# A recurrence beside a feed-forward layer: y and the state's products of steps six to eleven put into one place

## The chip, the core and the metric

The kernel runs on one core of a Trainium2 chip. The time is device time in microseconds (us) of the whole program, and a lower time is better. The engines of a core work on their own instruction streams, each in the order of its program, and wait for each other through semaphores: TensorE (PE in the profile, with its weight loads as PEld), VectorE (DVE), ScalarE (ACT), GpSimd (POOL), and SyncE (SP), which only starts DMA transfers here.

## The reference

There are two blocks. The first is a recurrence with a decay for every channel: 4 batches, 8 heads, 768 time steps, 48 channels a head.

```python
for t in range(S):
    cur = einsum('bhd,bhe->bhde', u * k[t], v[t])
    y[t] = einsum('bhd,bhde->bhe', r[t], state + cur)
    state = w[t][..., None] * state + einsum('bhd,bhe->bhde', k[t], v[t])
```

The second is a feed-forward layer on y, brought to 3072 tokens of 384 channels, with 2048 hidden channels:

```python
h = x @ w_in
g = h * erf(softplus(h))
out = g @ w_out
```

Everything is fp32.

## The kernel before

**The work is cut into twelve steps.** A step takes one chunk of 128 tokens of two batches, all heads. Even steps belong to one pair of batches, odd steps to the other, so a pair's state goes from step s to step s + 2. A chunk is two halves of 64 tokens, and in each the recurrence is worked out by levels: level n makes the part of the 64 x 64 table of token pairs that lies between neighbouring blocks of 2^(n-1) tokens, with r and k scaled by running products of the decays (`scale`, L364 in this path). The table is called `own`. From step five on, levels one to four come from VectorE and GpSimd on another layout (the rest of `prepare`, L486 to L568, "the row work"), and only levels five and six come from TensorE (`level_products`, L671). `take_level` brings a level from PSUM into `own`: level five by a predicated copy on VectorE (L681), level six by two copies on ScalarE (L688).

**y of a step comes in three parts**, all added up in one PSUM tile `y`: `from_own` (L703) multiplies `own` with v, once for each of two arrangements of the heads (swap 1 and swap 0); `through_state` (L729) adds r through the state at the chunk's start (S) and at its middle (`middle`). Between the two arrangements stands a fence: VectorE copies a few elements of `y` (L712), and the second arrangement has to wait for that copy. After that ScalarE copies `y` out (L737, L758), and SP's DMAs (L764) bring the last 16 channels of each into place, giving the layer's input xT. y of step s - 1 is finished in step s.

**The state** is advanced in two halves. `state_part` (L778) multiplies k (`kT`, multiplied beforehand by decays, L837) with v for both halves; then middle = faded S + first product (L857) and next state = faded middle + second product (L863), on VectorE. The fading, a multiplication with the chunk's decays, is GpSimd's (L832, L860), and both use one buffer, `faded`. kT comes by DMA (L617) from a copy in DRAM, behind two other transfers in SP's order (L609, L611), and is then multiplied by `spread`, decays that come by DMA (L802, L807) from products that TensorE makes with level six (L791).

**The feed-forward layer fills the rest.** In each step, TensorE computes the output projection of step s - 3 in seven products (P, L1275, each 8 matmuls of 128 x 192) and the hidden layer of step s - 1 in eight pieces (H, L1153, each 12 matmuls of 128 x 256). ScalarE copies the pieces out (L1162) and computes softplus (s, L1109) and erf (e, L1113); VectorE multiplies (m, L1118) and makes the blends that the projection uses (S1 to S4, L1252 to L1258). Two outputs are added on VectorE (L1295, L1300), and they free the PSUM buffers `m` that the hidden pieces then use.

**The order is written out by hand** in `attend_late` and in lists of tokens that it runs at named places:

```python
STAGES_LATE = ("front", "near", 0, 1, 2, 3, 4)
USUAL = ("s P", "m", "ey P m s P P ep P", "m k22y P F P k11p F F",
         "S1", "S2 S3 H k12y S4 H F", "s H ey m H H F s H ep H H")
```

F and `next(following, None)` advance the row work of the next step by one piece, up to its next `yield`. Each engine then takes its instructions in the order in which the program issues them.

**PSUM** has two banks of products in this path. Level five, level six with the spread, and the state's products all take bank 0 (`products(..., 0)`, called pp_107 or pp in the profile), one after the other; bank 1 serves ScalarE as a place for erf and copies.

Of the kernel before, what the change touches and what calls it, by code (L numbers as in the profile page):

```python
# [17 lines left out]
P = 128  # L18
# [3 lines left out]
HC = 64  # L22
NC = 2
# [17 lines left out]
DIRECT = 4  # L41
NEAR_LOG = 4
NEAR = 1 << NEAR_LOG
LOG = 6
# [47 lines left out]
def kernel(  # L92
# [14 lines left out]
    nc = tc.nc  # L107
    PSUM = bass.MemoryType.PSUM

    n_steps, _, _, JP, C = rkw.shape  # L110
    NH, D = v.shape[2:]
    NP = JP // NJ
    NE = NH // JP
# [5 lines left out]
    SPC = NB // NJ  # L119
# [20 lines left out]
    middle = const.tile([P, JP, D], FP32, name="middle")  # L140
    faded = [const.tile([P, JP, D], FP32, name="faded")] * NC
# [22 lines left out]
    def products(shape, n=None):  # L164

        if n is None:
            n = turns["next"]
            turns["next"] = 1 - n
        names = "abc"[: len(shape) - 1]
        return banks[n][:].rearrange(  # L170
            f"p ({' '.join(names)}) -> p {' '.join(names)}", **dict(zip(names, shape[1:]))
        )

    loaded = {}
# [165 lines left out]
    both = slice(0, EP + D)  # L340
# [7 lines left out]
    def scale(s, level, batch=None):  # L348

        in_t, tots = loaded[s][0], ready[s][1]  # L350
        half, nb = 1 << (level - 1), JP * C >> level
        if batch is not None:
            nb //= NJ
            halves = view(
                turns["first"][:, batch], half, [[NP * C - half, 2], [2 * half, nb], [1, half]]
            )
            nc.vector.tensor_mul(
                halves, halves,
                view(tots[level - 1], 2 * batch * nb, [[1, 2], [2, nb], [0, half]]),
            )  # L360
            return
        n = 1 if s > DIRECT and level == LOG else 2
        halves = view(in_t[:, 0:2], half, [[JP * C - half, n], [2 * half, nb], [1, half]])
        nc.vector.tensor_mul(  # L364
            halves, halves, view(tots[level - 1], 0, [[1, n], [2, nb], [0, half]])
        )
# [23 lines left out]
    def prepare(s):  # L390


        in_t = loaded[s][0]
        if s < DIRECT:
            rk1 = att.tile([P, 2, JP, C], FP32, name="rk1", bufs=1)
            ready[s] = (rk1,)
            parts = 1 if s else NJ
            def multiply_u(i, x):
                n = slice(i * JP // parts, (i + 1) * JP // parts)
                with_u, plain = (  # L400
                    [
                        t.rearrange("p n (t two) -> p n t two", two=2)[..., one]
                        for t in (rk1[:, x, n], in_t[:, x, n] if s else turns["first"][:, i, x])
                    ]
                    for one in (x, 1 - x)
                )
                if not s and not (x and not i):
                    nc.vector.tensor_mul(
                        with_u[0], with_u[1],
                        u_sb[:, :, None].to_broadcast([P, NP, C // 2]),  # L410
                    )
                    nc.vector.tensor_copy(out=plain[0], in_=plain[1])
                    return
                for p in range(NP):
                    of = slice(p, None, NP)
                    nc.scalar.mul(
                        out=with_u[0][:, of], in_=with_u[1][:, of], mul=u_sb[:, p : p + 1]
                    )
                nc.scalar.copy(plain[0], plain[1])

            if s < 2:
                for i in range(parts):
                    for x in range(2):
                        multiply_u(i, x)
                return
            yield
            yield
            multiply_u(0, 0)
# [21 lines left out]
        own = att.tile([P, NH, HC], FP32, name="own")  # L450
# [116 lines left out]
        fade(beside, k, 1)  # L567
        nc.vector.tensor_mul(own_terms, own_terms, r)  # L568
        fade(nc.vector, r, 1)
        if levels < NEAR_LOG:  # L570
            yield
        sum_up(1)
        multiply(nc.vector, 2)
# [103 lines left out]
    def take_level(own, pp, level):  # L677
        half = 1 << (level - 1)
        got = pp[:].rearrange("p e n t -> p (e n) t")
        if level <= MASKED:  # L680
            nc.vector.copy_predicated(  # L681
                rights(own[:], half),
                rights(mask_sb[:, level - 1 : level, :].to_broadcast([P, NH, HC]), half),
                got[..., : HC // 2].rearrange("p n (b h) -> p n b h", h=half),
            )
        else:
            for s0 in range(0, C, HC):
                nc.scalar.copy(own[s0 : s0 + half, :, half:], got[s0 : s0 + half, :, :half])  # L688
# [5 lines left out]
    def from_own(s, own, swap):  # L694
        vt = loaded[s][1]
        for j in range(NJ):
            for q in range(0, NP, 2):
                for h in range(NC):
                    e = h ^ swap
                    for p in (q, q + 1):  # L700
                        n = j * NP + p
                        t = slice(h * HC, (h + 1) * HC)
                        nc.tensor.matmul(  # L703
                            y[at(e, p), e, p // 2, j, t],
                            lhsT=vt[t, n * NE + e, :], rhs=own[t, e * JP + n, :],
                            start=swap == 1 and not j and not q, stop=True,
                            skip_group_check=True,
                        )
# [60 lines left out]
    def state_part(s, kT, ps, halves=None):  # L769

        vt = loaded[s][1]
        if halves is None:
            halves = range(1 if s >= n_steps - SPC else NC)
        for n in range(JP):
            for h in halves:
                for e in range(NE):
                    t = slice(h * HC, (h + 1) * HC)
                    nc.tensor.matmul(  # L778
                        ps[h][e][rows(e), n, :D],
                        lhsT=kT[t, e * JP + n, :],  # L780
                        rhs=vt[t, n * NE + e, :],
                        start=True,
                        stop=True,
                    )
# [27 lines left out]
    def attend_late(s, run):  # L812

        c, in_t, vt, own, S, S_next, ends = parts_of(s)
        RK = by_pair(in_t)
        before = s - 1 if s - 1 > DIRECT else None
        if before:
            from_own(before, ready[before][0], 1)
            fence()
        pp = products([P, NE, JP, HC], 0)  # L820
        level_products(pp, RK, LOG - 1)
        scale(s, LOG - 1)
        take_level(own, pp, LOG - 1)
        run("front", None)
        if before:
            from_own(before, ready[before][0], 0)
            through_state(before, xTs[before])
            if s + 1 < n_steps:
                load_step(s + 1)
        following = prepare(s + 1) if s + 1 < n_steps else iter(())  # L830
        next(following, None)
        nc.gpsimd.tensor_mul(faded[0][:], S[:], ends[:, :, 0:1].to_broadcast([P, JP, D]))  # L832
        next(following, None)
        run("near", None)
        next(following, None)
        kT = kTs[s]
        nc.vector.tensor_mul(  # L837
            kT[:].rearrange("p (e n) d -> p n e d", e=NE),
            kT[:].rearrange("p (e n) d -> p n e d", e=NE), spread[s][:],
        )  # L840
        run(0, following)

        pp = products([P, NE, JP, HC], 0)
        level_products(pp, RK, LOG)
        if s + 1 < n_steps:
            spread_blocks(s + 1, pp)
        take_level(own, pp, LOG)
        if s > DIRECT + 1:
            scale(s, LOG)
        run(1, following)  # L850
        if s == DIRECT + 1:
            scale(s, LOG)
        ps = products([P, NC, JP, HC], 0)
        ps = [[ps[:, h]] * NE for h in range(NC)]
        state_part(s, kT, ps)
        run(2, following)
        nc.vector.tensor_add(middle[both], faded[0][both], ps[0][0][both, :, :D])  # L857
        run(3, following)
        if s < n_steps - SPC:
            nc.gpsimd.tensor_mul(  # L860
                faded[1][:], middle[:], ends[:, :, 1:2].to_broadcast([P, JP, D])
            )
            nc.vector.tensor_add(S_next[both], faded[1][both], ps[1][0][both, :, :D])  # L863
        run(4, following)

    def attend_first(xT):
# [674 lines left out]
    with tc.manual_schedule(  # L1541
# [15 lines left out]
        for s in range(n_steps):  # L1557
# [44 lines left out]
            def run(n, following):  # L1602
                if n == 3 and s < n_steps - 2:
                    load_rows(s + 2)
                if n == 3 and s + 3 < n_steps:
                    load_w(s + 3)
                run_late(s, LATE.get(s, USUAL)[STAGES_LATE.index(n)], following)
# [120 lines left out]
```

## Time and profile before

| | us |
|---|---|
| median of 3 runs | 575.22 (575.20 to 575.34) |
| the profiled execution | 574.36 |
| its span, first to last instruction | 572.6 |
| TensorE busy in the span | 564.2 |
| VectorE, ScalarE, GpSimd busy | 452.7, 358.5, 246.8 |

The granted TensorE clock was 0.999 of full speed. Steps six to ten run from 232.7 to 454.25 us of the span, and step eleven from there to 477.8. In step seven (277.06 to 321.36) TensorE was busy for 44.30 us, VectorE for 37.41, ScalarE for 29.24 and GpSimd for 22.93.

In the profile, a row names the line, the engine, what was written and from what; "x64" counts instructions, and an fp32 matmul is two. The chain that ended last follows the work back from the last instruction to the first, so its rows, in order of time, tell what the time was spent on. A wait row reads: engine, what it was to write and its line, the releaser and its line, then the us in total, how often, and the longest. Times in the text are from the span's start.

### The profile page before, as it was taken

The numbers are of one execution on the slowest core, as the hardware profiler recorded it, in microseconds if no ns is written. First come the engines' busy times: TensorE is split into PE (matmuls) and PEld (weight loads), VectorE is DVE, ScalarE is ACT, GpSimd is POOL, SyncE is SP. The second block draws the span as 40 slices with busy tenths as digits, with TensorE's granted clock in tenths as the row PEclk, the third lists the DMA queues.
The fourth block names the chain that finished last, engine by engine and source line by source line (L and its number), as shares of the span: only waits on it lengthen the run. The fifth ranks groups of instructions, "written<-read, shape, count | busy, mean of one in ns | idle before, by whom it ended". The sixth has DMA issues, their size and how long they took to land.

```text
span 572.6 us, 16719 instructions
## 1 busy us (share of the span) xinstructions
PE 564.2 (99%) x7320; PEld 500.6 (87%) x7320; DVE 452.7 (79%) x506; ACT 358.5 (63%) x495; POOL 246.8 (43%) x265
## 2 busy tenths in 40 slices
PE   8899999999999999999999999999999999999997
PEld 5688887578998998998998998898898899989997
DVE  8774886999899899799699599599599596477730
ACT  3658877645458858747756766766675771489500
POOL 4557380731885884384285185176075000000000
PEclk9999999999999999999999999999999999999999
DMA  7596671440426324245245236234232201000000
GB/s 256 199 297 269 224 224 43 187 158 10 148 64 188 104 63 163 38 158 168 35 145 176 40 121 198 41 112 166 47 112 84 47 9 35 2 2 1 27 29 27
DMA packets 54082, 63.24 MB, mean 110 GB/s; under 512 B 35161, under 2 KB 40569, under 8 KB 52985
## 3 DMA queue, kind: packets, MB, share of 16 engines
q1 hardware_dynamic: 53624, 61.98, 34.4%
q8 instruction: 57, 0.93, 0.7%
q10 hardware_dynamic: 384, 0.20, 0.1%
q14 instruction: 17, 0.13, 0.1%
HBM read 52.39 MB, written 8.69 MB: 107 GB/s over the span
## 4 chain that ended last, share of the span: by engine, by line
PE 89%; DVE 5%; DMA 2%; ACT 1%; POOL 1%; issue 1%; SPq 0%; DVEq 0%; ACTq 0%; POOLq 0%
PE m L1275 33%; PE m L1153 32%; PE c L1378 6%; PE pp L671 5%; PE m L1185 4%; PE y L703 2%; PE y L729 2%; PE pp L778 2%; DVE in L364 1%; DMA words<-in_moe_w_in 1%; PE pp L990 1%; PE pp L1063 1%; DMA u_sb<-in_u 1%; DVE h L1118 1%; POOL tot_sb L386 0%
## 5 line engine op out<-in xcount | busy, mean ns | idle before, releaser
L1153 PE MATMUL m<-xT,w_in_sb 128*128 128x256 f32 x960 | 214.9, 382 | 0.2 <-ACT h L1162 0.2
L1153 PEld LDWEIGHTS m<-xT,w_in_sb 128*128 128x128 f32 x960 | 179.9, 190 | 25.5 <-ACT h L1162 0.6
L364 DVE TENSOR_TENSOR in<-in,tot_sb 128x1024 f32<-128x1024 f32 (+1 forms) x55 | 77.4, 1408 | 5.9 <-PE pp L671 3.4
L1162 ACT COPY h<-m 128x512 f32<-128x512 f32 x80 | 46.3, 580 | 47.8 <-PE m L1153 47.5
L1275 PE MATMUL m<-mixed,h 128*128 128x192 f32 x320 | 56.7, 331 | 0.0
L1275 PE MATMUL m<-w_out_sb,h 128*128 128x192 f32 x320 | 56.2, 329 | 0.0
L1275 PEld LDWEIGHTS m<-mixed,h 128*128 128x128 f32 x320 | 51.8, 190 | 0.9
L1275 PEld LDWEIGHTS m<-w_out_sb,h 128*128 128x128 f32 x320 | 52.0, 190 | 0.5
L1275 PE MATMUL m<-w_out_sb,room 128*128 128x192 f32 x288 | 49.7, 326 | 0.0
L1275 PEld LDWEIGHTS m<-w_out_sb,room 128*128 128x128 f32 x288 | 47.3, 190 | 0.1
L1113 ACT ACT_TABLE_LOAD x28 | 35.9, 1283 | 10.5 <-DVE h L1118 8.4
L534 POOL TENSOR_TENSOR words<-words 128x384 f32<-128x384 f32 x28 | 39.7, 1448 | 0.0
L671 PEld LDWEIGHTS pp<-in 48*48 48x48 f32 (+4 forms) x2368 | 30.1, 120 | 10.9 <-issue 5.8
L493 POOL TENSOR_TENSOR words<-words,own 128x384 f32<-128x384 f32 x21 | 30.1, 1433 | 22.0 <-DVE words L524 13.0
L1109 ACT ACT_TABLE_LOAD x28 | 35.9, 1283 | 1.8 <-issue 1.3
L486 POOL TENSOR_TENSOR own<-rest 128x384 f32<-128x384 f32 x7 | 9.7, 1384 | 61.0 <-ACT o L1281 61.0
L671 PE MATMUL pp<-in 48*48 48x32 f32 (+4 forms) x2368 | 34.0, 206 | 0.3 <-DVE in L364 0.3
L534 POOL TENSOR_TENSOR rk<-words 128x384 f32<-128x384 f32 x28 | 33.4, 1225 | 0.0
L559 DVE TENSOR_REDUCE sums<-rk 128x16 f32<-128x768 f32 (+2 forms) x31 | 31.6, 1021 | 0.0
L438 POOL TENSOR_TENSOR tot_sb<-tot_sb 128x256 f32<-128x256 f32 (+4 forms) x50 | 29.9, 598 | 3.8
L1109 ACT ACTIVATE room<-h 128x1024 f32<-128x1024 f32 x28 | 29.6, 1057 | 0.3
L319 POOL TENSOR_TENSOR w_out_sb<-w_out_sb,rest 128x768 int32<-128x768 int32 x8 | 18.3, 2290 | 21.9 <-DVE w_out_sb L311 21.9
(214 smaller groups left out, 1008.7 us busy)
## 6 DMA issues: line engine op xcount, KB each, us to landing
in<-in_rkw SPq DMA_DIRECT2D x8, 1024.0 KB, 5.3
words<-in_moe_w_in SPq DMA_DIRECT2D x16, 384.0 KB, 6.3
words<-in_moe_w_out SPq DMA_DIRECT2D x16, 384.0 KB, 4.4
words<-in_rk_rows SPq DMA_DIRECT2D x8, 768.0 KB, 6.4
w<-in_rkw SPq DMA_DIRECT2D x11, 512.0 KB
v<-in_v SPq DMA_DIRECT2D x12, 384.0 KB, 5.7
out<-o SPq DMA_DIRECT2D x23, 192.0 KB, 3.0
in<-in_rkw SPq DMA_DIRECT2D x7, 512.0 KB, 5.9
```

Of the source, the lines that this page charges most:

```text
L364: nc.vector.tensor_mul(halves, halves, view(tots[level - 1], 0, [[1, n], [2, nb], [0, half]]))
L438: nc.gpsimd.tensor_mul(new, pair[:, :, 0], pair[:, :, 1])
L493: engine.tensor_mul(to, to, of[:, :, None, :].to_broadcast([P, NEAR // 2 // half, half, D]))
L534: engine.tensor_mul(to[:, i], r[:, half:], k[:, part * rows + i, None].to_broadcast([P, half, D]),)
L559: nc.vector.tensor_reduce(out=to, in_=of, axis=mybir.AxisListType.X, op=ALU.add)
L671: nc.tensor.matmul(to, lhsT=rk(1, n)[rows(e), s0 : s0 + m], rhs=right, start=True, stop=True,)
L1109: nc.scalar.activation(sp_room, chunks[0], AF.Softplus)
L1113: nc.scalar.activation(at, sp_room, AF.Erf)
L1153: nc.tensor.matmul(ps[:, ff, :], lhsT=w_in_sb[:, g * FG + f + ff, kk * P : (kk + 1) * P], rhs=xT[:, kk, :], start=kk == 0, stop=kk == KT - 1,)
L1162: nc.scalar.copy(h[:, f : f + FT, :], ps[:])
L1275: nc.tensor.matmul(to, lhsT=a[:, f], rhs=b[:, f], start=start and f == 0, stop=f == FG - 1, skip_group_check=True,)
L1378: nc.tensor.matmul(to[:, f], lhsT=turns["weights"][b][:, i * FT + f], rhs=turns["tokens"][a], start=a + b in STARTS and not f, stop=True, ...
```

## The change

For steps six to eleven (where `before` is set):

- Both arrangements of y from the chunk, level five, y through the state, and now the state's products stand together on TensorE. The first projection product of the step (P of "s P"), which stood between level five and the second arrangement, comes behind them.
- Level five's copy into `own` comes ahead of its scaling.
- K times decays comes at the beginning of the step's instructions, ahead of the fence; so does the fading of S, now ahead of the next step's totals on GpSimd.
- middle, its fading and the next state follow the state's products at the front of the step.
- The row work of steps seven to eleven gets one more `yield`, so that the next state stands between two of its pieces.
- ScalarE copies y out ahead of the step's first output copy (L1281).

Steps up to five keep their order. Every engine has as many instructions as before, and SP's have the same order.

```diff
@@ in prepare
-        if levels < NEAR_LOG:
+        if levels < NEAR_LOG or s > DIRECT + 2:
             yield
...
@@ in attend_late
+        following = prepare(s + 1) if s + 1 < n_steps else iter(())
+        kT = kTs[s]
+
+        def fade_state(h, of):
+            nc.gpsimd.tensor_mul(
+                faded[h][:], of[:], ends[:, :, h : h + 1].to_broadcast([P, JP, D])
+            )
+
+        def fade_k():
+            nc.vector.tensor_mul(
+                kT[:].rearrange("p (e n) d -> p n e d", e=NE),
+                kT[:].rearrange("p (e n) d -> p n e d", e=NE), spread[s][:],
+            )
+
+        def state_products():
+            ps = products([P, NC, JP, HC], 0)
+            state_part(s, kT, [[ps[:, h]] * NE for h in range(NC)])
+            return ps
+
+        def next_middle(ps):
+            nc.vector.tensor_add(middle[both], faded[0][both], ps[both, 0, :, :D])
+
+        def next_state(ps):
+            if s < n_steps - SPC:
+                nc.vector.tensor_add(S_next[both], faded[1][both], ps[both, 1, :, :D])
+
         if before:
+            fade_k()
+            fade_state(0, S)
+            next(following, None)
             from_own(before, ready[before][0], 1)
             fence()
         pp = products([P, NE, JP, HC], 0)
         level_products(pp, RK, LOG - 1)
-        scale(s, LOG - 1)
-        take_level(own, pp, LOG - 1)
-        run("front", None)
         if before:
+            take_level(own, pp, LOG - 1)
+            scale(s, LOG - 1)
+        else:
+            scale(s, LOG - 1)
+            take_level(own, pp, LOG - 1)
+        if before:
+            run_late(s, "s")
             from_own(before, ready[before][0], 0)
             through_state(before, xTs[before])
             if s + 1 < n_steps:
                 load_step(s + 1)
-        following = prepare(s + 1) if s + 1 < n_steps else iter(())
-        next(following, None)
-        nc.gpsimd.tensor_mul(faded[0][:], S[:], ends[:, :, 0:1].to_broadcast([P, JP, D]))
+            ps = state_products()
+            next_middle(ps)
+            if s < n_steps - SPC:
+                fade_state(1, middle)
+            run_late(s, "P")
+            next(following, None)
+            next_state(ps)
+        else:
+            run("front", None)
+            next(following, None)
+            fade_state(0, S)
         next(following, None)
         run("near", None)
         next(following, None)
-        kT = kTs[s]
-        nc.vector.tensor_mul(
-            kT[:].rearrange("p (e n) d -> p n e d", e=NE),
-            kT[:].rearrange("p (e n) d -> p n e d", e=NE), spread[s][:],
-        )
+        if not before:
+            fade_k()
         run(0, following)
...
-        ps = products([P, NC, JP, HC], 0)
-        ps = [[ps[:, h]] * NE for h in range(NC)]
-        state_part(s, kT, ps)
+            ps = state_products()
         run(2, following)
-        nc.vector.tensor_add(middle[both], faded[0][both], ps[0][0][both, :, :D])
+        if not before:
+            next_middle(ps)
         run(3, following)
-        if s < n_steps - SPC:
-            nc.gpsimd.tensor_mul(
-                faded[1][:], middle[:], ends[:, :, 1:2].to_broadcast([P, JP, D])
-            )
-            nc.vector.tensor_add(S_next[both], faded[1][both], ps[1][0][both, :, :D])
+        if not before:
+            fade_state(1, middle)
+            next_state(ps)
         run(4, following)
```

## The prediction

> **What bounds the kernel now.** I read the page's first part, then the waits of steps six to eleven, then the chain that ended last.
>
> ```profile
> PE 564.2 (99%) x7320; PEld 500.6 (87%) x7320; DVE 452.7 (79%) x506; ACT 358.5 (63%) x495; POOL 246.8 (43%) x265
> ```
>
> TensorE is busy for 99% of the span, so nothing that shortens another engine's work helps by itself. The time changes only if TensorE's own stream gets shorter or gets holes. The waits between 232 and 477 us:
>
> ```profile
> DVE seen L712 <- PE y L703: 19.3, 6, 3.6
> ...
> DVE own L633 <- DMA by_tokens<-by_blocks: 11.4, 5, 2.8
> ...
> PEld y L703 <- issue: 3.3, 12, 0.3
> ...
> PEld pp L778 <- ACT y L1233: 1.1, 5, 0.2
> ```
>
> No PE row is among them: TensorE waits for nobody in six steps. VectorE waits for TensorE, some 3.5 us a step ahead of the fence (L712). The chain through step seven, which starts at 277.06 us (start, duration, work), and through the end of step eleven:
>
> ```profile
> 277.06 0.59 PE y L703 x32
> 277.65 0.71 PE pp L671 x64
> 278.36 2.80 PE m L1275 x16
> 281.16 0.59 PE y L703 x32
> 281.75 0.90 PE y L729 x64
> 282.65 10.60 PE m L1275 x64
> 293.25 0.69 PE pp L671 x50
> 294.18 5.40 PE m L1275 x32
> 299.58 0.86 PE pp L778 x64
> 300.44 20.92 PE m L1153 x96
> ...
> 476.52 0.81 PE pp L778 x30
> 477.37 0.45 PE y L703 x30
> ```
>
> The reader should see that a step is 44.30 us of TensorE (the gap at 293.94 is the spread, L791, 0.24), and the same in steps six to ten; and that four groups of small tiles (y, pp) lie between large ones (m).
>
> **What a change of kind costs.** The projection's groups take 2.80, 5.40, 8.00, 10.60 and 13.20 us for 16, 32, 48, 64 and 80 instructions. That is 2.60 per 16 and 0.20 left over once for each group, whatever its length. The hidden layer's groups are 2.59 per 12 with the same rest: 20.92 for 96 behind the state's products, but 5.18 for 24 at 165.34 us, straight behind a projection. So 0.20 goes with a small group ahead of a large one. The small groups have a surcharge too: L703 takes 0.59 behind a large group and 0.45 behind the state's products (477.37); L729 takes 1.04 behind a large group (189.19) and 0.90 behind L703. That is 0.14. A round trip from large to small and back therefore costs 0.34 us above the work itself.
>
> [...]
>
> **The change, part by part.**
>
> *TensorE.* Today a step has four small groups: y and level five; y and state; level six with the spread; the state's products. Afterwards it has two: y, level five, y, state and products in one; level six with the spread. Two round trips go, 0.68 us. A step by the rows: 0.59 + 0.71 + 0.45 + 0.90 + 0.72 (0.86 less 0.14), then five products in one run 13.20, level six and spread 0.93, two products 5.40, hidden straight behind them 20.72 (20.92 less 0.20): 43.62 against 44.30. This holds for steps six to ten, 5 x 0.68 = 3.40. Step eleven has no hidden layer behind its state products, but the y group of the closing part, which joins them today at 0.45 and will cost 0.59: one round trip, 0.34. Together 11 round trips, **3.74 us**. No instruction is added or dropped on any engine. Two seams are in no row: level five to y, and state to products. Each lies between 0.14 more (as behind a large group) and 0.10 less (a fifth of a 0.45 group, run into its neighbour). I take 0, as in the seams L703 to L671 and L703 to L729 that the rows show.
>
> *The fence comes close.* The second y (L703) waits for the fence, today 3.5 us behind the first, afterwards 0.71. The fence starts 0.07 after the first y and ends at 277.89. A weight load began 0.06 after the DVE instruction that it waited for (47.19 to 47.25), so it could go at 277.95. Level five, without the change to large behind it, ends at about 278.2. Level five covers it, by 0.2 us.
>
> *Bank 0.* The state's products reuse the bank of level five, so they wait for VectorE's copy out of it, which now goes ahead of the scaling. It starts where the scaling starts today, 278.43, takes 0.71 and ends at 279.14. The products are due at 277.06 + 0.59 + 0.71 + 0.45 + 0.90 = 279.71. Covered by y and state, 0.5 us.
>
> *VectorE.* middle (0.46 net) and the next state (0.46) move to the front, with 0.3 of waiting for the products; the row work is cut in two and follows. K times decays (1.24 net) leaves the middle, so around the outputs' additions VectorE is about where it is today, and from there 0.5 early. The one deadline is the first hidden tile, now due 22.9 us into the step: its PSUM buffer is freed by L1295, which ends near 21.3. K times decays then runs at the step's end, into the 3.5 us ahead of the fence. What is queued behind it is the fence, and behind the fence TensorE. In step seven K is issued at 314.61 and lands 4.6 later, at 319.2 or 42.1 into the step; with 0.95 (step eleven) to 1.33 us (step seven) it ends by 43.5, and the fence is due 43.62 + 0.65 = 44.27. Cover 0.8 us, plus the 0.2 of level five. At step six K is issued at 227.39, landing at about 232.1; it ends between 233.0 and 233.4, the fence's present start: up to 0.1, once.
>
> *GpSimd.* The fading of middle goes ahead of the row work, which queues behind it: it can start at 3.9 into the step and ends at 4.8; the row work (L486) starts at 281.92 today, 4.86 in. No loss. The fading of S goes ahead of the totals, which are needed 10 us later.
>
> *ScalarE and the queues.* The y copies go ahead of the first output copy (L1281, 0.32), and run 3 us earlier; that copy is next needed three products later. SP's order is unchanged; the xT parts and the load of the next step are issued about 3 us sooner. Nothing.
>
> **Sum.** The profiled execution took 574.36 us (span 572.6): 574.36 - 3.74 = 570.6. The timed runs' median, 575.22, lies 0.86 above it, so I state 575.22 - 3.74 = **571.5 us**.
>
> **The rivals.**
>
> *A wait is laid bare.* A matmul that TensorE had to hold for VectorE came 0.24 us late (L729 behind middle, at 23.72). If the fence's 0.2 us cover is not enough, 6 x 0.24 = 1.4 comes back: 572.9. For it: that cover is thin. Against: the fence ends before level five does. If the products wait too, 2.9 comes back: 574.4, no difference that can be told.
>
> *Only part of the surcharge goes.* If the 0.20 belongs to the start of any long run and not to the small group ahead, only 0.14 a round trip goes: 11 x 0.14 = 1.5, 573.7. Against: five rows with 0.20 whatever the length, and 5.18 without it behind a large group. [...]
>
> *Slower: K's landing holds the fence.* Beyond about 1.0 us of delay, each further us of K's landing is one us of idle TensorE in each of six steps. The loss overtakes the gain and 1.15 us more from a delay of 1.0 + (3.74 + 1.15) / 6 = 1.8 us. At 2.5 it would be 6 x 1.5 - 3.74 = 5.3 above: 580.5. For it: K is now in front of the fence in a queue that works in order, and its DMA waits in SP's queue behind two others. Against: it lands at much the same place in each step, and VectorE asks for it slightly earlier.
>
> **How the numbers follow.** Forecast 0.72 (571.5; with the two unseen seams 11 x 0.10 below to 11 x 0.14 above, 570.4 to 573.0). One wait bare 0.09 (572.9). Only part 0.05 (573.7). Both waits bare 0.08 (574.4). Slower 0.06 (580.5). The range 570.4 to 573.8 takes in the first three. A measurement of this kernel can tell about 0.2%, 1.15 us: faster 0.72 + 0.09 + 0.05 = 0.86, same 0.08, slower 0.06.
>
> **What would show it.** In the chain of the changed kernel, steps six to ten should be 43.6 us long; y should read 0.59 then 0.45, the state's products about 0.72, one run of 13.20 for 80 projection instructions, and a hidden run of about 20.7 straight behind 5.4. No PE row should appear among the waits of these steps. A PE row "y L703 <- DVE seen" or "pp L778 <- DVE own" shows the first rival, and a fence that starts more than 0.1 behind the first y the last one; a run of 13.20 with 20.9 for hidden, the second. The prediction is wrong if the step stays above 44 us.

## The result, and the profile after

The changed kernel is slower: its median is 582.68 us (five runs, 581.04 to 585.30) beside 575.22 of the kernel before, a ratio of 1.0137 with a 95% interval of 1.0103 to 1.0171. The forecast was 571.5. The profiled execution took 581.82 us, with a span of 580.0 and a mean granted clock of 0.997.

The first part of the page after, the line that answers to the one shown of before:

```profile
PE 563.4 (97%) x7320; PEld 502.6 (87%) x7320; DVE 450.6 (78%) x506; ACT 359.0 (62%) x495; POOL 253.3 (44%) x265
```

TensorE is busy 0.8 us less than before (564.2), where the forecast asked for 3.74 less, and the span is 7.4 longer. So most of the lost time is in holes of TensorE, and about 3 us in longer work, both told below. The waits of steps six to eleven (232 to 484 us), where before had no PE row:

```profile
PE y L729 <- issue: 4.3, 3, 1.5
PE pp L778 <- issue: 4.3, 3, 1.7
```

Six holes, one in each step, 8.6 us together. Neither row names an engine. "issue" is time in which TensorE waited for nothing that the profile shows: no semaphore, no buffer, no transfer of data. The rows that the prediction had named as signs of its first rival ("y L703 <- DVE seen", "pp L778 <- DVE own") are absent. The chain through step seven of the changed kernel:

```profile
277.57 0.59 PE y L703 x32
278.17 0.70 PE pp L671 x64
278.87 0.46 PE y L703 x32
279.33 0.90 PE y L729 x64
280.23 0.36 PE pp L778 x32
280.59 1.74 issue
282.33 0.57 PE pp L778 x32
282.90 13.20 PE m L1310 x80
296.10 0.69 PE pp L671 x50
297.04 5.40 PE m L1310 x32
302.43 20.72 PE m L1188 x96
```

Nearly every term of the forecast stands in it: y 0.59 and then 0.46, one projection run of 13.20, a hidden run of 20.72 straight behind 5.40. (L1310 and L1188 are the projection and the hidden layer, L1275 and L1153 before.) What the sum did not have is the row of "issue". TensorE does half of the state's products, stops for 1.74 us, and does the other half.

From the first y of step six to the end of the closing part's y it was 245.06 us before, should have been 245.06 - 3.74 = 241.32, and is 252.98 (232.39 to 485.37): 11.66 too much. By steps, six to eleven, the excess is 1.56, 1.96, 1.45, 1.72, 3.31 and 1.65. The "issue" rows of the chain are 1.31, 1.74, 1.20, 1.41, 1.46 and 1.43 of it. In five of the steps the other 0.22 to 0.31 goes with the interrupted group, which seems to pay for its start twice: the products of step seven take 0.36 and 0.57 in their two parts, 0.93 together, and 0.72 in one piece. In step ten a further 1.62 is another thing. The first projection run behind the hole took 14.82 instead of 13.20, and the windows show why (length, then busy time and instructions of PE, PEld, DVE, ACT, POOL, then the granted clock, DMA share and GB/s):

```profile
418.50:420.00 1.50, 1.50 (x11) 1.46 (x6) 1.28 (x2) 0.72 (x3) 0.00 (x0) 0.50 0.07 19
420.00:421.50 1.50, 1.50 (x6) 1.50 (x5) 1.48 (x3) 0.00 (x0) 0.81 (x1) 0.50 0.09 25
```

The granted clock is 0.50 for 3.41 us, from 418.46 to 421.88, which takes 0.003 off the mean of the span. Four of the five runs of the changed kernel have such a mean, 0.996 or 0.997, and the longest (585.30 us) has 0.994, room for two such stretches.

**What is missing in a hole.** The page lists a DMA queue of the kind "instruction":

```profile
q8 instruction: 57, 0.93, 0.7%
```

TensorE has 14,640 instructions (7320 matmul instructions, from here on called matmuls, and as many weight loads). Divided by 57 transfers that is 257 each, and 0.93 MB by 14,640 is 64 bytes. From these numbers the author estimates that the queue brings TensorE's instructions, and that a transfer of 16 KB (0.93 MB by 57) is one piece of 256 of them, or 128 matmuls. No row says so; the places of the holes, below, agree with it. The packets of this queue in step seven start at 279.56 (1.43 long, until 280.99) and at 283.49. TensorE stops at 280.59 and goes on at 282.33, 1.34 behind the end of the first one. In step six the transfer ends at 235.61 and TensorE resumes at 236.99, 1.38 behind; in step ten at 415.76 and 417.22, 1.46 behind. In step ten no other transfer was under way, and the transfer took 0.93.

### The profile page after: what moved, and what is told of

Its sections match the earlier page's. It is cut to its first block, busy times and chain, and to the rows that moved or that the text cites. A ratio compares the mean times of both kernels' runs of the same rounds, so it can differ in the third digit from the quotient of the medians.

```text
span 580.0 us, 16722 instructions
## 1 busy us (share of the span) xinstructions
PE 563.4 (97%) x7320; PEld 502.6 (87%) x7320; DVE 450.6 (78%) x506; ACT 359.0 (62%) x495; POOL 253.3 (44%) x265
## 4 chain that ended last, share of the span: by engine, by line
PE 91%; DVE 4%; issue 2%; ACT 1%; DMA 1%; SPq 0%; DVEq 0%; ACTq 0%
PE m L1188 34%; PE m L1310 33%; PE c L1413 6%; PE pp L671 6%; PE m L1220 4%; PE y L703 2%; PE y L729 2%; PE pp L778 2%; DVE in L364 1%; PE pp L1025 1%; PE pp L1098 1%; DMA u_sb<-in_u 1%; DVE h L1153 1%; PE c L1310 0%; PE m L1016 0%
## 5 line engine op out<-in xcount | busy, mean ns | idle before, releaser
L1188 PE MATMUL m<-xT,w_in_sb 128*128 128x256 f32 x960 | 214.4, 381 | 0.2 <-ACT h L1197 0.2
L1188 PEld LDWEIGHTS m<-xT,w_in_sb 128*128 128x128 f32 x960 | 180.2, 190 | 25.2 <-ACT h L1197 0.6
L1197 ACT COPY h<-m 128x512 f32<-128x512 f32 x80 | 46.2, 580 | 44.3 <-PE m L1188 44.0
L1310 PE MATMUL m<-w_out_sb,h 128*128 128x192 f32 x320 | 57.8, 336 | 0.0
L1310 PE MATMUL m<-mixed,h 128*128 128x192 f32 x320 | 56.1, 329 | 0.0
L1310 PEld LDWEIGHTS m<-w_out_sb,h 128*128 128x128 f32 x320 | 53.6, 195 | 0.5
L1310 PEld LDWEIGHTS m<-mixed,h 128*128 128x128 f32 x320 | 52.1, 190 | 0.4
L1310 PE MATMUL m<-w_out_sb,room 128*128 128x192 f32 x288 | 49.7, 326 | 0.0
L1310 PEld LDWEIGHTS m<-w_out_sb,room 128*128 128x128 f32 x288 | 47.3, 190 | 0.1
L534 POOL TENSOR_TENSOR words<-words 128x384 f32<-128x384 f32 x28 | 42.6, 1554 | 0.0
L821 POOL TENSOR_TENSOR faded<-middle,tot_sb 128x384 f32<-128x384 f32 x5 | 12.1, 2421 | 60.9 <-DVE middle L837 60.9
L438 POOL TENSOR_TENSOR tot_sb<-tot_sb 128x256 f32<-128x256 f32 (+4 forms) x50 | 31.8, 636 | 3.8
L534 POOL TENSOR_TENSOR rk<-words 128x384 f32<-128x384 f32 x28 | 29.9, 1095 | 0.0
L1316 ACT COPY o<-m 128x192 f32<-128x192 f32 x11 | 3.5, 316 | 39.9 <-PE m L1310 39.9
```

The lines of the kernel that those rows point to most:

```text
L438: nc.gpsimd.tensor_mul(new, pair[:, :, 0], pair[:, :, 1])
L534: engine.tensor_mul(to[:, i], r[:, half:], k[:, part * rows + i, None].to_broadcast([P, half, D]),)
L1188: nc.tensor.matmul(ps[:, ff, :], lhsT=w_in_sb[:, g * FG + f + ff, kk * P : (kk + 1) * P], rhs=xT[:, kk, :], start=kk == 0, stop=kk == KT - 1,)
L1197: nc.scalar.copy(h[:, f : f + FT, :], ps[:])
L1310: nc.tensor.matmul(to, lhsT=a[:, f], rhs=b[:, f], start=start and f == 0, stop=f == FG - 1, skip_group_check=True,)
```

## The experiments

**The first theory (T1)** is that TensorE outruns its instruction supply. A piece of 128 small matmuls is used up in about 1.65 us (1.66 in the run with the products three times), while TensorE goes on only 2.2 to 2.8 us behind the start of the transfer in the six holes (2.53, 2.77 and 2.39 in the three steps above). Counted back from the holes, the transfer starts 0.6 to 0.9 us behind the first matmul of the piece before in each of the six steps. The changed kernel puts 256 small matmuls in one row (224 in steps ten and eleven), which always hold most of a whole piece. Before, no row of small ones in these steps was over 96 matmuls, and 16 large ones (2.80 us) or more stood between two of them. **The rival (T2)** is that something at this place of the step holds TensorE, whatever the number of matmuls: the fence, the copy out of bank 0, K or the state's products themselves, in a way the wait rows miss. Under T1, the place of the hole moves with the count of instructions, since a step has 532 matmuls, 20 over four pieces; under T2 it stays with an operation. In the changed kernel it moves: the hole comes behind the 246th matmul of the block in step six, then behind the 224th, 201st, 179th, 157th and (step eleven is put together otherwise) 166th.

**The block cut in two.** The first projection product goes back between the second y and y through the state: small blocks of 128 matmuls (the second has 96 in steps ten and eleven), with 16 large between them.

```diff
             from_own(before, ready[before][0], 0)
+            run_late(s, "P")
             through_state(before, xTs[before])
...
-            run_late(s, "P")
             next(following, None)
             next_state(ps)
```

> As the changed kernel, but the first projection product of the step stands between the second y arrangement and y through the state, so that the small tiles come as 128 (y, level five, y) and 128 (state, state's products) instructions with 16 large ones between. Theory 1 (TensorE's instructions come in pieces of 128 matmuls with their weight loads, and a piece run through in less than some 3.3 us is ahead of the next one's arrival; the place of the piece's end moves up by some 20 matmuls from step to step, from the 118th of step six): no piece lies wholly in small tiles in any of the six steps, no hole, granted clock as before, and one round trip of 0.34 us saved in each of steps six to ten: 573.5 us. Theory 2 (TensorE is held by VectorE: the copy of level five out of bank 0, the fence, or K times decays): the state's products have 2.8 us more behind the copy, the fence is as close: 573.5 too if only the copy is it, 580 or more if the fence or K is it, with the holes at the same instruction in each step.

Measured: 584.85 us, ratio 1.0181 (1.0158 to 1.0204). The holes were gone as T1 says, and the time was no better. The waits of the same stretch have one PE row worth naming:

```profile
PE m L1188 <- DVE o L1330: 6.4, 5, 1.6
```

This is another wait, and one that the prediction had called harmless. The first hidden tile waits for VectorE's last addition of outputs, the deadline that the prediction had put at 22.9 us into the step, with VectorE due at 21.3. In step seven L1330 starts at 304.75 and takes 0.54, and the tile goes at 305.35, 1.55 late. Its run of 96 then takes 21.63 in place of 20.72, because further tiles wait for ScalarE's copies behind it (PEld m L1188 <- ACT h L1197: 5.2 us in all). Together that is 2.46 in each of steps six to nine; in step ten, where the tile was 0.21 late, it is 1.11. This makes 10.95, against 11.35 between 584.85 and the expected 573.5.

Why VectorE is late: middle came later than in the changed kernel (behind 2.80 us of projection), everything on VectorE behind it too, and GpSimd's fading of middle, ahead of the row work, took far longer than its row before. From GpSimd's timeline:

```profile
287.64 2.82 POOL L821 TENSOR_TENSOR faded<-middle,tot_sb 128x384 f32<-128x384 f32 x1 [18.28 <-DVE middle L837]
```

The same instruction took 0.834 to 0.836 us in the kernel before, where it ran beside VectorE's work on PSUM (in step seven from 305.75, beside L1254 from 305.59, which reads `pp`). Here it starts 0.16 behind the first of three VectorE instructions with two SBUF operands (L565 at 287.48 for 0.95, L515 at 288.34 for 0.55, L568 at 288.81 for 0.95), and it ends 0.70 after the last of them (290.46 and 289.76), nearly its own full length. In the changed kernel it was as long, 2.82, and began 0.17 behind L565 (283.68 and 283.51). The author's reading of these times is that it was held until the three were through; what held it is in no row.

**The same, with 32 more small matmuls far ahead.** In step three, level five is computed for four pairs once more, which shifts all later pieces by 32 matmuls and costs little itself.

```diff
                 level_products(pp, rk, level)
+            if (s, level) == (DIRECT - 1, LOG - 1):
+                level_products(pp, rk, level, range(4))
```

> The same as the split kernel, with half of level five's products of step three issued twice (32 more small TensorE instructions, 0.35 us, same values), so that every piece of instructions ends 32 matmuls earlier from there on. Theory 1: piece ends now fall so that a piece lies nearly wholly in small tiles in steps nine and ten: holes of about 1.1 and 1.5 us there and none in the others: 573.5 + 0.35 + 2.6 = 576.5 us, plus 1.7 if a hole trips the clock. Theory 2: nothing depends on the count: 573.9 us, no hole that the split kernel has not.

Measured: 583.55 us, ratio 1.0168 (1.0152 to 1.0183), with the waits of the kernel just told and no hole. The expectation of a hole in a block of 128 was wrong: in step nine, for which one had been expected, the transfers start at 371.12 and 374.83, each ahead of its block (371.69 and 376.25). By the author's reading of these times, a hole needs a block that is longer than the pieces at hand.

**The changed kernel, with the same 32 more.** Nothing near the block is touched.

> The changed kernel, with the same 32 extra small TensorE instructions in step three. Theory 1: six holes remain, one a step, of 1.2 to 1.8 us, and each stands 32 matmuls earlier in its small block: about the 214th instead of the 246th in step six, the 194th in step seven, so in the state's products no longer late but early, and in the second y or the state in steps nine to eleven: 582 to 586 us as the changed kernel, by how often the clock trips. Theory 2: holes stay at the instruction at which they stand now.

Measured: 577.32 us, ratio 1.0049 (1.0032 to 1.0065). The holes came 32 earlier in their blocks, as forecast (behind the 214th matmul in step six, the 192nd in seven, 170th in eight and 147th in nine, where 0.31 was left of it). Counted from the first matmul of the program they did not move: they stand behind 3914, 4424, 4934 and 5443 matmuls, and in the changed kernel behind 3914, 4424, 4933 and 5443, though other operations stand there. In steps ten and eleven there was none. This was not forecast, and the packets say why. In step ten the transfer starts at 411.19, during the hidden layer's large matmuls and 2.60 us ahead of the block (in the changed kernel at 414.83, 1.27 into it). By the count, the piece before begins 2 matmuls ahead of the block here, and at the 30th matmul of the block in the changed kernel. The last part of the block there, which began at 413.79:

```profile
415.09 0.46 PE y L703 x32
415.55 0.90 PE y L729 x64
416.45 0.71 PE pp L778 x32
417.16 13.20 PE m L1312 x80
```

The same order of work, the same instructions, with no hole. From the first y (413.79) to the next one (457.40) it is 43.61 us, and the forecast had 43.62. T2 falls: the same operations at the same place lose nothing when the transfer comes earlier. This is also the cleanest proof of the forecast's price for a change of kind.

**Only y joined.** The kernel before, with both arrangements of y, level five and y through the state in one place, and the state's products left where they were: a block of 192.

```diff
-        run("front", None)
         if before:
+            run_late(s, "s")
             from_own(before, ready[before][0], 0)
             through_state(before, xTs[before])
             if s + 1 < n_steps:
                 load_step(s + 1)
+            run_late(s, "P")
+        else:
+            run("front", None)
```

> The kernel before with only the first half of the change: y, level five, y and y through the state stand together (192 small matmuls), the first projection product behind them; the state's products, K times decays and VectorE's order stay where they were. Theory 1: a piece of 128 lies wholly in the block only where its end falls in the first 74 matmuls or so: holes in steps nine, ten and eleven, at about the 179th, 159th and 171st matmul, and none in steps six to eight. One round trip saved in each of six steps (2.0), three holes of 1.5: 575.2 - 2.0 + 4.5 = 577.7 us, plus 1.7 for each trip of the clock. Theory 2 (fence): holes in all six steps, ahead of the second y; if bank 0 or K is the cause: none, 573.2.

Measured: 577.82 us, ratio 1.0078 (1.0050 to 1.0107). By T1 a hole at about the 246th, 224th or 200th matmul lies beyond a block of 192, so steps six to eight should have none. The chain in steps seven and ten:

```profile
278.93 0.90 PE y L729 x64
279.82 13.20 PE m L1278 x80
...
413.08 1.43 issue
414.51 0.77 PE y L729 x37
```

Steps six to eight had none, steps nine to eleven had one each (1.50, 1.43, 1.16), just as expected, behind 5442, 5951 and 6460 matmuls of the program (5443, 5953 and 6462 in the changed kernel). The holes now stand in y through the state, and the state's products, K and middle are where they were before. They have no part in it.

**Only K ahead.** The kernel before, with K times decays moved ahead of the first y, and nothing else.

```diff
         if before:
+            fade_k()
             from_own(before, ready[before][0], 1)
             fence()
...
-        nc.vector.tensor_mul(
...
+        if not before:
+            fade_k()
```

> The kernel before with one part of the change alone: K times decays at the end of the step, ahead of the fence. Theory 1 (this part is harmless, the holes are TensorE's own): 574.3 us, no wait of TensorE in steps six to eleven, fence within 0.1 us behind the first y. Theory 2 (K's landing in front of the fence is what costs): 578 or more, TensorE held at the second y.

Measured: 574.16 us, ratio 0.9999 (0.9984 to 1.0014). K in front of the fence costs nothing here. A projection product still stands between the two y in this kernel, so the second y had some 3 us to spare; that K costs nothing with the fence close is read from the changed kernel's own trace (below).

**The state's products three times.** The changed kernel, with the products of steps six to eleven repeated, 384 small matmuls in one block.

```diff
-            state_part(s, kT, [[ps[:, h]] * NE for h in range(NC)])
+            for _ in range(3 if before else 1):
+                state_part(s, kT, [[ps[:, h]] * NE for h in range(NC)])
```

> The changed kernel, with the state's products issued three times in steps six to eleven (same values; 128 more small matmuls in steps six to nine, 64 in ten and eleven). Theory 1: the small block of steps six to nine is 384 matmuls, so a second piece end falls 128 behind the first, and there is a second hole of 1.5 to 1.9 us in each of these steps: about 1.44 of work and 1.7 of hole a step, some 600 us in all with a trip or two of the clock. Theory 2 (a dependency holds TensorE once): 1.44 us a step in steps six to nine and 1.4 in ten and eleven, 592 us, one hole a step.

Measured: 606.17 us, ratio 1.0554 (1.0511 to 1.0597). The chain in step seven:

```profile
287.16 1.09 issue
288.26 1.66 PE pp L778 x128
289.91 1.80 issue
291.71 0.57 PE pp L778 x32
```

Measured time is above the 600 expected: there are eleven holes, 17.6 us together (step ten has two as well, step eleven one), and the profiled run, at a mean granted clock of 0.992, has two projection runs of 14.88 in place of 13.20 (in steps seven and nine, behind holes of 1.80 and 1.86), as behind the hole of step ten in the changed kernel. Between the two holes of a step lie 128 matmuls (127 in step ten), as many as the estimate from the page's 57 transfers gave for a piece, and they take 1.66 us. From one resumption to the next it is 3.45 us (288.26 to 291.71), and 4.28 in step six (239.28 to 243.56): 128 matmuls per 3.45 to 4.3 us, under T1 the pace of the supply. The transfers here start at 286.03, 289.36 and 293.07, 3.33 and 3.71 apart.

**Without y through the state.** The changed kernel leaves out `through_state` for the y of steps five to ten, 64 small matmuls of the block.

```diff
-            if not (c or h):
+            if not (c or h) or DIRECT < s < n_steps - 1:
                 continue
```

> The changed kernel without y through the state of steps five to ten (that part is left out of the result), so 64 small matmuls less a step: the block is 192 in steps six to nine and 160 in ten and eleven. Theory 1: a piece no longer lies wholly in the block in every step. A step now has 468 matmuls, so the piece ends move down by some 42 a step; a hole follows only where they fall at the 18th to 74th (18th to 42nd in steps ten and eleven): steps seven and ten, perhaps eight, none in six, nine and eleven. Theory 2 (fence, copy of level five or K): as the products now come 0.9 us sooner behind the copy, a hole in each step, at the state's products.

Measured: 571.86 us, ratio 0.9959 (0.9938 to 0.9980). Holes came in steps seven and ten alone (0.82 and 1.11), as expected from the count. With this cover gone, a wait that the prediction had worked out as covered by 0.5 us is laid bare:

```profile
PE pp L778 <- DVE own L681: 2.2, 6, 0.4
```

**The block cut in two, with both causes seen to.** As the first experiment, and the first piece of row work goes ahead of middle and its fading, the next state behind the second piece. So L565, L515 and L568 on VectorE are through (283.18 in step seven) when GpSimd's fading of middle begins (285.00).

```diff
             from_own(before, ready[before][0], 0)
+            run_late(s, "P")
             through_state(before, xTs[before])
...
             ps = state_products()
+            next(following, None)
             next_middle(ps)
...
-            run_late(s, "P")
-            next(following, None)
-            next_state(ps)
...
         next(following, None)
+        if before:
+            next_state(ps)
```

> The split kernel with the first piece of row work (VectorE L565 to L493, GpSimd L486 and L493) put ahead of middle and its fading, and the next state behind the second piece. Theory 1 with its second part (in the split kernel TensorE lost nothing to holes in its instructions, but 1.55 us a step at the first hidden tile, because middle came 3.2 us later and GpSimd's fading of middle took 2.82 instead of 0.83 us beside VectorE's row work): the row work now fills VectorE's wait for the state's products, L1330 ends some 22 us into the step and the first hidden tile is due at 23.3: no wait, no hole, a step of 43.96 against 44.30 us in steps six to ten: 574.3 - 1.7 = 572.6 us, lower than the kernel before. Theory 2 (VectorE's new order itself costs, whatever stands where): the wait at the hidden tile stays, 580 or more.

Measured: 572.94 us (12 runs) beside 573.99 (28 runs), ratio 0.9978 (0.9960 to 0.9996). This is faster than both kernels, by 0.2% against the kernel before: 1.05 us, where 1.7 had been expected. The chain of step seven (from 276.95), and then GpSimd's timeline there:

```profile
278.71 2.80 PE m L1311 x16
281.51 1.04 PE y L729 x64
282.55 0.72 PE pp L778 x64
283.27 10.60 PE m L1311 x64
```

```profile
285.00 0.84 POOL L821 TENSOR_TENSOR faded<-middle,tot_sb 128x384 f32<-128x384 f32 x1 [0.96 <-DVE middle L837]
```

No hole, and no PE wait but one of 0.2 us. The products stand in one piece, the fading of middle is back at 0.84 us, and the step is 43.97 us (276.95 to 320.92), with 43.96 expected: one round trip of 0.34 saved, 44.30 - 0.34. The changed kernel's other round trip asks for a block of 256, and such a block had a hole in each of its steps six to nine.

## Why the prediction was wrong

**The step that failed** is the sum's own frame: "TensorE waits for nobody in six steps", so its time is its rows and its waits for other engines. The supply of instructions that T1 reads from the holes is not in the rows of these steps before, where every row of small matmuls was short (96 at most) and followed by at least 2.80 us of large ones. The change made the block long enough to use up a piece of 128 in 1.65 us, and in its holes TensorE went on only 2.2 to 2.8 us behind the start of the transfer. Six holes cost 10.0 us (11.66 less 1.62), against a gain of 3.74. Two independent runs show it: the count shifted by 32 takes the holes away in two steps and puts them elsewhere in the others, and three times the products gives two holes a step with 128 matmuls between. Leaving the state's y in or out, and joining y alone, each moved the holes to the steps that the count names.

The trace of the kernel before shows such a hole once, outside the steps that the prediction read:

```profile
PE pp L671 <- issue: 0.8, 1, 0.8
```

It stands near the start of the program, where small matmuls also follow each other closely. TensorE stops at 27.12 us and goes on at 27.88, 1.37 behind the end of a transfer of the instruction queue (26.51). And in steps eight to ten of the kernel before, by the same count, the first matmul of a new piece ran only 2.2 us behind the end of its transfer; the holes of all these runs ended 1.2 to 1.6 behind it.

**The clock.** 1.62 us of the excess is a granted clock of 0.50 for 3.41 us behind the hole of step ten, which the prediction had no term for. What starts it is open. This stretch followed a hole of 1.46 us, and the two long projection runs with the products three times followed holes of 1.80 and 1.86. But holes of 1.74 (step seven of the changed kernel), 2.62 and 2.08 (steps six and eight with the products three times) had a projection run of 13.20 behind them, and one of the 28 runs of the kernel before has a mean clock of 0.996.

**What a change of kind costs: right.** 0.34 a round trip, 0.68 a step: 43.61 us where no hole fell, with 43.62 forecast, and 43.97 with one round trip less. The second rival ("only part of the surcharge goes") falls.

**The two unseen seams: right.** Level five to y and state to products were taken as 0 beside their rows; the rows 0.46, 0.90 and 0.71 of the step without holes bear it out to 0.01 us each.

**The fence, bank 0 and K: right.** No PE row names L712, L681 or L826 in the changed kernel (one weight load, of the first y in step seven, waited 0.3 us for L826, and no matmul did). The fence started 0.07 behind the first y in each of the six steps, as forecast, and VectorE had been idle before it, for 0.42 us in step six and 1.07 in step seven, so K at the head of its queue held nothing; alone, K measured 0.9999. The first and third rivals fall. That bank 0 was covered by y through the state is shown by the run without it (a wait of 0.4 in each step).

**GpSimd: wrong in size.** The prediction gave the fading of middle 0.83 us and said "No loss". It took 2.82 beside VectorE's row work; the row it was priced from stood beside instructions on PSUM. In the changed kernel no PE wait shows it. In the block cut in two, with middle some 3 us later, it may have helped to lay bare the deadline of the first hidden tile: 5 waits, 6.4 us. VectorE's cover at this tile was smaller than the 1.6 us of the prediction (22.9 less 21.3): 1.1 in step seven of the changed kernel (L1330 ends at 301.34, the tile runs from 302.43), with the fading at 2.82 there too. The 2.80 us that middle came later, less the 0.34 that the tile was due later, exceed that cover by 1.4, an estimate from these numbers for the 1.55 measured. What GpSimd alone would cost was not measured apart; undoing both by the order of the row work took all of it away.

Of the forecast's rivals, one was a smaller price for a change of kind, and the others were waits for another engine. None had the holes that decided.

**Open:** why TensorE goes on only 1.2 to 1.6 us behind the end of a transfer, what asks for the next one, and what starts the clock of 0.50. The block without its first y and level five (y through the state and the products alone, behind a projection product) was not run.

## What to carry to other kernels

In these runs TensorE stopped for 0.6 to 2.6 us in long blocks of small matmuls, which neither its busy share nor the waits of the steps to be changed showed beforehand: before joining groups of small matmuls into one, count how many stand between large ones, and put the count against the size of an instruction piece (here, by the estimate, 128 matmuls with their weight loads, one per 3.45 to 4.3 us). Blocks up to that length lost nothing here; cut a longer one with a few large matmuls, as the last experiment did. And the duration of a row holds for its neighbours: an instruction on GpSimd that is moved must be priced by what VectorE does beside it at the new place (here 2.82 us against 0.83).

## What the runs showed of the hardware

- Blocks of 224 and 256 small matmuls had a hole in each of six steps of the changed kernel and in four of six with 32 more matmuls far ahead, of 192 in three of six, of 160 to 192 (without the state's y) in two of six, of 128 in none, and of 288 and 384 twice in five steps and once in the sixth. A hole is 0.6 to 2.6 us (0.31 where the transfer began early). TensorE goes on 1.2 to 1.6 us behind the end of a transfer of the instruction queue.
- Where a hole falls depends on the number of all matmuls ahead of it in the program: with 32 more in step three the holes stayed behind the same count (3914, 4424, 4934, 5443), two were gone, and the ratio went from 1.0137 to 1.0049, in a kernel otherwise equal.
- The granted clock fell to 0.50 for 3.41 us, 1.24 us behind the end of a hole of 1.46 us (417.22 to 418.46). The mean clock of all five runs (0.994 to 0.997) suggests at least one such stretch in each; of the kernel before, one of 28 runs had a mean below 0.999, and of the last experiment, two of twelve. The longest idle time of TensorE between its first and last matmul in this trace is 1.74 us.
- A GpSimd multiplication that began 0.16 to 0.17 us behind the first of three VectorE instructions with two SBUF operands took 2.82 us; beside VectorE's work on PSUM it took 0.83, and begun after the three it took 0.84.
